# A reordered first batch, shifted pieces and later query loads in a cosformer attention and mixer kernel

## The chip, the cores and the metric

The kernel runs on one core of a Trainium2 chip. Its engines work side by side, each through its own list of instructions in order: PE (TensorE, matmuls, with its weight loads listed as PEld), DVE (VectorE), ACT (ScalarE), POOL (GpSimd) and SP (SyncE, which here only issues transfers). Sixteen DMA engines move data. The metric is the device time of one execution in microseconds (us), as the median of several runs.

## The reference

Inputs are q, k and v of shape 8 x 8 x 576 x 64 (batch, heads, sequence, head width) and four weight matrices. Attention is linear: a feature map, two sums over the sequence, a quotient. Then comes a mixer over tokens and one over channels.

```python
def phi(x, c, s):
    r = np.maximum(x, 0.0)
    return np.concatenate([r * c, r * s], axis=-1)
q_p, k_p = phi(q, cos_w, sin_w), phi(k, cos_w, sin_w)   # cos, sin of pi/2 * pos / 576
kv = np.einsum('bhsf,bhsd->bhfd', k_p, v)
z = np.sum(k_p, axis=2)
num = np.einsum('bhsf,bhfd->bhsd', q_p, kv)
den = np.einsum('bhsf,bhf->bhs', q_p, z)[..., None] + 1e-06
x = (num / den)                                          # to (batch, 576, 512)
h = np.maximum(x.transpose(0, 2, 1) @ w_tok1, 0.0) @ w_tok2
u = x + h.transpose(0, 2, 1)
out = u + np.maximum(u @ w_ch1, 0.0) @ w_ch2             # w_ch1 512x1536, w_ch2 1536x512
```

## The kernel before, in words

The 576 positions of a batch are four full chunks of 128 (ci 0 to 3) and a tail of 64 (ci = R = 4). The tails of two batches share one set of 128-row tiles (the class Tail): the even batch has rows 0 to 63, the odd one rows 64 to 127.

Each batch has a front and a channel part. The front makes the features (`feature`, by `k_side` and `q_side`: one cosine and one sine operation for a chunk), casts the values into `v_aug` with a column of ones (`values`), transposes the query features (`q_trans` on PE, or `q_trans_dma` by a DMA that SP issues), sums kv (`kv`, copied out by `kv_out`), forms the numerator (`num`, which ends in the DVE operation that writes x), and mixes tokens (`tok1`, `tok1_out`, `tok2`, which writes u; `u_trans_dma` then transposes u). The channel part (class Channel) has twelve `c_main` steps, each four matmuls and a relu on ACT into h1T, and then o steps of two matmuls each, whose sums DVE adds to u and SP stores.

The order is written out by hand; nothing reorders it. The first batch's front (`first_front`) runs alone at the start, with filler matmuls (`busy`) that keep PE occupied. After it, while one batch's channel part runs, the pieces of the next batch's front are issued between its steps: `pieces` returns a plan of (slot, what, arguments), where the slot counts the channel steps (C = 0 for the c_main steps, O = 12 for the o steps), and the main loop calls them after that step. A negative slot lies at the end of the batch before. The plan has one form for the second batch (`first`), one for the third (`late`), one for odd and one for even batches. Whatever is issued takes its place in its engine's list, so a piece that waits holds up what stands behind it on that engine, though not other engines.

Loads are issued by SP, one also by ACT at the start, and the casting loads of the channel weights by POOL. The main loop places the loads of later batches by step number (`load_batch`, at the end of the kernel). SP also issues the stores and the DMA transposes, so these too stand in its order. Every buffer is a pool tile with a fixed number of copies: four PSUM tiles of one bank (`ps_mm`), two of two banks (`ps_at`); a matmul group waits until the tile's last reader is done.

In the first batch's front the denominators of all chunks are computed ahead, from the key sums (`ksum`, `ksum_out`, `dens`, `dens_out`): dens of three chunks, then the first half (four heads) of kv, then dens of the other two, then the second half of kv. The two token weights are loaded as f32 into buffers that later hold u, and are cast (`cast_tok1`) or permuted (`permute_tok2`) on ACT; the tail rows of the first token weight come by two casting loads on POOL (L183). The fills of ones and zeros of both copies of `v_aug` and `x_tail` are on DVE (L158 to L163).

The lines of the plan that the text refers to most are those of the second batch:

```python
plan = [(4, KS, 0), (4, KS, 1), (5, u, 0, ps_at, False), (5, KS, 2, True),
        (6, KS, 3, True), (6, u, 1, ps_at, False), (7, KS, R), (7, V, R, nc.vector), (8, V, 0, act),
        (8, V, 2, pool), (8, load_w_ch2, 0), (8, V, 3, pool),
        (8, load_w_ch2, 1), (8, load_w_ch2, 2),
        (8, u, 2, None, False), (9, V, 1, act), (9, u, 3, None, False),
        (9, QS, 0), (10, u, R, None, False)]
```

Here `u` is the first batch's own `tok2`: its u is finished beside its own channel part, since its channel input was formed on PE directly (`turned_x`, `turned_b`).

Of the kernel before, what the change touches and what calls it, by code (L numbers as in the profile page):

```python
# [16 lines left out]
def kernel(  # L17
# [137 lines left out]
    v_augs, x_tails = [], []  # L155
    for i in range(2):
        va = const.tile([P, NSC, H, DP], BF16, name=f"v_aug{i}")
        nc.vector.memset(va[:, 0:R, :, D:D1], 1.0)  # L158
        nc.vector.memset(va[half(1 - i), R, :, :], 0.0)
        nc.vector.memset(va[half(i), R, :, D:D1], 1.0)  # L160
        v_augs.append(va)
        xt = const.tile([P, Dm], BF16, name=f"x_tail{i}")
        nc.vector.memset(xt[half(1 - i), :], 0.0)  # L163
        x_tails.append(xt)
# [29 lines left out]
    def load_w_ch2(third):  # L194
        ki = third * NCH // 3
        w_ch2_done.append(nc.gpsimd.dma_start(
            out=w_ch2[:, ki:ki + 4, :],
            in_=moe_w_ch2[ki * P:(ki + 4) * P, :].rearrange("(n t) d -> t n d", t=P)))
# [10 lines left out]
    def permute_tok2(ki):  # L209
        nc.scalar.copy(w_tok2[:, ki, 0:SM].rearrange("t (r p) -> t r p", r=R),  # L210
                       w_tok2n[:, ki, 0:SM].rearrange("t (p r) -> t r p", r=R))
        nc.scalar.copy(w_tok2[:, ki, SM:].rearrange("t (g s) -> t g s", g=2),
                       w_tok2n[:, ki, None, SM:S].to_broadcast([P, 2, ST]))


    class Front:
        def __init__(self, b, res, tail):
            self.qt, self.vt, self.kt = io_tiles[b]
            self.va, self.xt = v_augs[b % 2], x_tails[b % 2]
            self.res, self.tail = res, tail  # L220
            self.rows = half(b % 2)


            self.alone = b < 2
            self.kp, self.qp = {}, {}
# [69 lines left out]
        def dens(self, ci):  # L295

            if ci == 0:
                self.d_ps = ps_mm.tile([P, NSC * H], F32, name="d_ps", tag="mm")
                self.d_sb = small.tile([P, NSC * H, 1], F32, name="d_sb")
            for h in range(H):  # L300
                i = ci * H + h
                nc.tensor.matmul(self.d_ps[:, i:i + 1], self.qT_of(ci, h),
                                 self.ks_sb[:, h:h + 1], start=True, stop=True)

        def dens_out(self, lo, hi):
            nc.vector.tensor_scalar_add(self.d_sb[:, lo:hi, 0], self.d_ps[:, lo:hi], 1e-6)
            nc.vector.reciprocal(self.d_sb[:, lo:hi, 0], self.d_sb[:, lo:hi, 0])

        def kv(self, ci, halves=(0, 1)):
            if ci == 0 and not hasattr(self, "kv_ps"):  # L310
                self.kv_ps = {}
                if halves == (0, 1):
                    both = ps_at.tile([P, 2, 512], F32, name="kv_ps", tag="at")
                    self.kv_ps = {g: both[:, g, :] for g in range(2)}
            if ci == 0 and halves != (0, 1):
                for g in halves:
                    self.kv_ps[g] = ps_at.tile([P, 2, 512], F32, name="kv_ps", tag="at")[:, 0, :]
# [10 lines left out]
        def kv_out(self, halves=(0, 1)):  # L328
            for g in halves:
                copy = nc.vector.tensor_copy if g else nc.scalar.copy  # L330
                copy(self.kv_sb[g][:, :, 0:D1],  # L331
                     self.kv_ps[g][:, 0:HH * DP]
                     .rearrange("p (j d) -> p j d", d=DP)[:, :, 0:D1])
# [13 lines left out]

        def q_trans_dma(self, ci):
# [4 lines left out]
        def num(self, ci, fill=0, dens=False):  # L353
            num_ps = ps_at.tile([P, 2, 512], F32, name="num_ps", tag="at")
            if fill:
                busy(num_ps[:, 0, HH * DP:512], 1)
            for h in range(H):
                g, j = divmod(h, HH)
                nc.tensor.matmul(num_ps[:, g, j * DP:j * DP + D1], self.qT_of(ci, h),  # L359
                                 self.kv_sb[g][:, j, 0:D1], start=True, stop=True)  # L360
            rows = self.rows_of(ci)
            nv = num_ps[rows, :, 0:HH * DP].rearrange("p g (j d) -> p g j d", d=DP)
            if dens:
                den = self.d_sb[rows, ci * H:(ci + 1) * H, :].rearrange("p (g j) o -> p g j o", g=2)
            else:
# [3 lines left out]
            nc.vector.tensor_mul(  # L369
                self.x_of(ci)[rows].rearrange("p (g j d) -> p g j d", g=2, j=HH),  # L370
                nv[:, :, :, 0:D], den.to_broadcast([rows.stop - rows.start, 2, HH, D]))
# [89 lines left out]
        def pieces(self, b, before):  # L461
# [7 lines left out]
            if first:  # L469

                u, act, pool = before.tok2, nc.scalar, nc.gpsimd
                plan = [(4, KS, 0), (4, KS, 1), (5, u, 0, ps_at, False), (5, KS, 2, True),
                        (6, KS, 3, True), (6, u, 1, ps_at, False), (7, KS, R), (7, V, R, nc.vector), (8, V, 0, act),
                        (8, V, 2, pool), (8, load_w_ch2, 0), (8, V, 3, pool),
                        (8, load_w_ch2, 1), (8, load_w_ch2, 2),
                        (8, u, 2, None, False), (9, V, 1, act), (9, u, 3, None, False),
                        (9, QS, 0), (10, u, R, None, False)]
# [6 lines left out]
            else:  # L484
                plan = [(C + at, V, ci, nc.scalar)
                        for ci, at in enumerate((6, 6, 7, 7, 7) if late else (-1, -1, 0, 1, 2))]

                if odd:
# [8 lines left out]
                for at, side, ci in sides:  # L497
                    plan.append((C + at, side, ci))
                    if side == QS:
# [3 lines left out]
                         enumerate((7, 7, 8, 8, 8) if late else  # L503
# [28 lines left out]
    class Channel:  # L532
# [59 lines left out]
        def steps(self, done):  # L592
# [43 lines left out]
    def first_front(f):  # L636
# [26 lines left out]
        busy(idle_ps, 1)  # L663
        for ci in range(R):
            if ci == 2:
                f.ksum_out()
            f.values(ci, nc.scalar, lo_heads)
        cast_tok1(0)
        f.values(R, nc.vector)
        for ci in range(R):  # L670
            f.values(ci, nc.vector, hi_heads)
        for ci in (0, 1, 2):
            f.dens(ci)
# [15 lines left out]
        f.num(ORDER[0], fill=1, dens=True)  # L689
        f.num(ORDER[1], dens=True)  # L690
# [57 lines left out]
    for b in range(B):  # L748
# [4 lines left out]
        for i, step in enumerate(steps):  # L753
# [54 lines left out]
```

## Time and profile before

| what | value |
|---|---|
| median of three runs | 270.0 us (269.47 to 270.21) |
| the profiled execution | 270.61 us |
| its span | 268.8 us |
| PE busy | 260.0 us, 97% |
| DVE busy | 164.9 us, 61% |
| ACT busy | 129.9 us, 48% |
| POOL busy | 10.9 us, 4% |
| DMA queue of SP | 49.62 MB, 69.5% of the 16 engines' span |
| granted PE clock | full speed throughout |

The span is what the profile shows; the profiled execution's own time is 1.80 us more, and 0.61 us above the median. A busy PE is not PE at its peak, since the ends of its matmuls are modelled; but steps that follow each other without a wait show how long a stretch must take. A wait is given in brackets behind a row with what ended it. A row with a count above one merges instructions that follow each other on one engine.

### The profile page before, as it was taken

The numbers are of one execution on the slowest core, as the hardware profiler recorded it, in microseconds if no ns is written. First come the engines' busy times: TensorE is split into PE (matmuls) and PEld (weight loads), VectorE is DVE, ScalarE is ACT, GpSimd is POOL, SyncE is SP. The second block draws the span as 40 slices with busy tenths as digits, with TensorE's granted clock in tenths as the row PEclk, the third lists the DMA queues.
The fourth block names the chain that finished last, engine by engine and source line by source line (L and its number), as shares of the span: only waits on it lengthen the run. The fifth ranks groups of instructions, "written<-read, shape, count | busy, mean of one in ns | idle before, by whom it ended". The sixth has DMA issues, their size and how long they took to land.

```text
span 268.8 us, 5101 instructions
## 1 busy us (share of the span) xinstructions
PE 260.0 (97%) x2029; PEld 139.2 (52%) x2050; DVE 164.9 (61%) x376; ACT 129.9 (48%) x228; POOL 10.9 (4%) x24
## 2 busy tenths in 40 slices
PE   7989999999999999999999999999999999999994
PEld 2565465455544455446644455446644455445543
DVE  6874798794366747777466747776565846720022
ACT  4954975528606272446606372546606362526400
POOL 6300220000000000000000000000000000000000
PEclk9999999999999999999999999999999999999999
DMA  6999999589999999469984989189974580180032
GB/s 217 342 277 275 333 162 285 211 210 253 179 316 289 251 208 319 146 166 266 182 307 117 287 207 355 54 179 254 229 261 117 156 120 0 53 202 3 2 107 88
DMA packets 91815, 53.68 MB, mean 200 GB/s; under 512 B 59408, under 2 KB 86928, under 8 KB 91792
## 3 DMA queue, kind: packets, MB, share of 16 engines
q1 hardware_dynamic: 88432, 49.62, 69.5%
q0 software_dynamic: 2832, 3.21, 7.2%
q10 hardware_dynamic: 528, 0.52, 0.6%
q8 instruction: 16, 0.26, 0.4%
q14 instruction: 7, 0.06, 0.1%
HBM read 35.85 MB, written 9.44 MB: 168 GB/s over the span
## 4 chain that ended last, share of the span: by engine, by line
PE 86%; DVE 6%; DMA 3%; ACT 3%; issue 1%; DVEq 0%; ACTq 0%
PE o_ps L579 33%; PE c_ps L546 25%; PE u_ps L406 7%; PE b_ps L382 6%; PE ct_ps L566 3%; PE kv_ps L320 3%; PE num_ps L359 3%; DVE x_sb L369 3%; DMA qt<-in_q_dram 2%; DVE qp L263 1%; ACT h1T L550 1%; PE qT_ps L340 1%; DMA qpT_tail<-qp_tail 1%; PE idle_ps L204 1%; ACT v_aug L274 1%; PE c_ps L556 1%
## 5 line engine op out<-in xcount | busy, mean ns | idle before, releaser
L579 PE MATMUL o_ps<-w_ch,h1T 128*128 128x512 bf16 (+1 forms) x380 | 92.6, 372 | 0.6
L546 PE MATMUL c_ps<-uT,w_ch 128*128 128x512 bf16 (+2 forms) x384 | 92.2, 372 | 0.1
L550 ACT ACTIVATE h1T<-c_ps 128x512 bf16<-128x512 f32 x93 | 55.5, 599 | 60.5 <-PE c_ps L546 60.1
L579 PEld LDWEIGHTS <-h1T 128*128 128x128 bf16 x396 | 37.3, 98 | 39.5 <-issue 0.2
L546 PEld LDWEIGHTS <-w_ch 128*128 128x128 bf16 x384 | 33.5, 97 | 29.5 <-issue 0.2
L584 DVE TENSOR_TENSOR o_sb<-o_ps,u_sb 128x512 f32<-128x512 f32 (+1 forms) x33 | 22.3, 674 | 29.5 <-PE o_ps L579 29.4
L409 DVE TENSOR_TENSOR u_sb<-u_ps,x_sb 128x512 f32<-128x512 f32 x32 | 21.7, 689 | 6.0 <-PE u_ps L406 5.6
L413 ACT CAST u_bf<-u_sb 128x512 bf16<-128x512 f32 x28 | 17.3, 620 | 16.7 <-DVE u_sb L409 16.7
L406 PE MATMUL u_ps<-B,w_tok 128*128 128x512 bf16 x79 | 22.4, 379 | 0.2
L387 ACT ACTIVATE B<-b_ps 128x512 bf16<-128x512 f32 x8 | 4.8, 598 | 33.7 <-PE b_ps L382 33.5
L369 DVE TENSOR_TENSOR x_sb<-num_ps,den 128x512 bf16<-128x512 f32 x28 | 19.4, 691 | 1.0
L566 PEld LDWEIGHTS <-w_ch 128*128 128x128 bf16 x192 | 14.0, 98 | 9.2
L382 PE MATMUL b_ps<-x_sb,w_tok 128*128 128x512 bf16 x63 | 17.7, 379 | 0.1
L263 DVE TENSOR_SCALAR kp<-kt,cos_t 128x512 bf16<-128x512 f32 x32 | 15.2, 481 | 3.8 <-DMA kt<-in_k_dram 3.8
L566 PE MATMUL ct_ps<-uT_tail,w_ch 128*128 128x128 bf16 x192 | 17.2, 219 | 0.0
L274 ACT CAST v_aug<-vt 128x512 bf16<-128x512 f32 (+1 forms) x30 | 16.8, 587 | 0.1
L263 DVE TENSOR_SCALAR qp<-qt,cos_t 128x512 bf16<-128x512 f32 (+1 forms) x35 | 15.9, 455 | 0.5 <-DMA qt<-in_q_dram 0.5
L263 DVE TENSOR_SCALAR qp<-qt,sin_t 128x512 bf16<-128x512 f32 (+1 forms) x35 | 15.9, 455 | 0.0
L359 PEld LDWEIGHTS <-qpT 128*128 128x128 bf16 x256 | 11.5, 98 | 6.1 <-issue 1.1
L584 DVE TENSOR_TENSOR o_sb<-o_ps,u_tail 128x512 f32<-128x512 f32 x4 | 2.8, 692 | 19.0 <-PE o_ps L579 19.0
L359 PE MATMUL num_ps<-kv_sb,qpT 128*128 128x65 bf16 x256 | 13.0, 193 | 1.3 <-DVE x_sb L369 0.5
L331 DVE CAST kv_sb<-kv_ps 128x260 bf16<-128x260 f32 x8 | 3.5, 433 | 16.6 <-ACT kv_sb L331 16.5
(93 smaller groups left out, 228.6 us busy)
## 6 DMA issues: line engine op xcount, KB each, us to landing
out_dram<-o_sb SPq DMA_DIRECT2D x31, 256.0 KB, 2.9
kt<-in_k_dram SPq DMA_DIRECT2D x7, 1024.0 KB, 6.6
vt<-in_v_dram SPq DMA_DIRECT2D x7, 1024.0 KB, 6.6
qt<-in_q_dram SPq DMA_DIRECT2D x7, 1024.0 KB, 8.4
w_ch<-in_moe_w_ch_dram POOLq DMA_DIRECT2D x4, 384.0 KB, 10.2
w_ch<-in_moe_w_ch_dram POOLq DMA_DIRECT2D x3, 512.0 KB, 7.5
out_dram<-o_sb SPq DMA_DIRECT2D x10, 128.0 KB, 2.3
qtt<-in_q_dram SPq DMA_DIRECT2D x8, 128.0 KB, 5.3
```

What stands on the lines that cost most here:

```text
L263: nc.vector.tensor_scalar(o_ap, i_ap, scalar1=w, scalar2=0.0, op0=ALU.mult, op1=ALU.max)
L274: nc.scalar.copy(dst, src)
L359: nc.tensor.matmul(num_ps[:, g, j * DP:j * DP + D1], self.qT_of(ci, h), self.kv_sb[g][:, j, 0:D1], start=True, stop=True)
L369: nc.vector.tensor_mul(self.x_of(ci)[rows].rearrange("p (g j d) -> p g j d", g=2, j=HH), nv[:, :, :, 0:D], den.to_broadcast([rows.stop - r ...
L382: nc.tensor.matmul(self.b1_ps[mi], w, self.x_of(ci), start=(ci == ORDER[0]), stop=(ci == ORDER[-1]))
L406: nc.tensor.matmul(u_ps, w_tok2[:, ki, ci * P:(ci + 1) * P], self.B1[:, ki, :], start=(ki == 0), stop=(ki == NT - 1))
L409: nc.vector.tensor_add(u, u_ps[rows], self.x_of(ci)[rows])
L546: nc.tensor.matmul(c_ps[:, lo:hi], w_ch1[:, ki, mi * P:(mi + 1) * P], uT[:, lo // P:hi // P, ki, :], start=(ki == 0), stop=(ki == NCC - 1))
L550: nc.scalar.activation(self.h1T[:, mi, :], c_ps, AF.Relu)
L566: nc.tensor.matmul(self.ct_ps[:, mi % R, :], w_ch1[:, ki, mi * P:(mi + 1) * P], self.tail.uT[:, ki, :], start=(mi % R == 0 and ki == 0), s ...
L579: nc.tensor.matmul(o_ps, h, w_ch2[:, ki, cols], start=ki == 0, stop=ki == NCH - 1)
L584: nc.vector.tensor_add(o_sb, o_ps, u)
```

## The change

It has three parts.

In the first batch's front: the tail rows of the first token weight are loaded by SP as f32, behind the main part and ahead of the second token weight, and cast by POOL. Half of the second token weight is permuted by POOL instead of ACT, and the fixed fills of the second `v_aug` and `x_tail` move from DVE to POOL, after that. The tail's queries are transposed on 64 rows only. The sine features of key chunks 1 to 3, instead of 2 and 3, are on ACT. Filler matmuls are fewer between key sums. The values of chunks 0 and 1 are cast on DVE and of 2 and 3 on ACT. All dens are computed in one go ahead of both kv halves, the kv halves have PSUM tiles of their own, both are copied out by ACT, and the nums of the first two chunks are formed by halves, the first of them in `ps_mm` tiles.

In the plans: the second batch's key, value and first query pieces come one or more slots later, behind u pieces of the first batch, which come earlier. The second channel weight is loaded in four pieces instead of three, and the first batch's o steps alternate after every step instead of every second one. The third batch's values and kv come one or two slots earlier. The fourth batch has all its key features before its query features, and these later.

In the loads: the third batch's value tails come with its values, its query tails later, in the second batch's stage; the fourth batch's queries are loaded in that stage's o steps, and the fifth batch's keys at the second step of the third batch's channel part.

```diff
@@ the first loads
+    w_tail1n = stage1[:, R * D_tok:(R + 1) * D_tok]
     nc.sync.dma_start(out=w_tok1n, in_=moe_w_tok1[0:SM, :].rearrange("(p r) t -> p r t", r=R))
+    for g in range(2):
+        nc.sync.dma_start(out=w_tail1n[half(g), :], in_=moe_w_tok1[SM:S, :])
     nc.sync.dma_start(out=w_tok2n, in_=moe_w_tok2.rearrange("(n t) s -> t n s", t=P))
...
-    for t in (tail0.kp, tail0.qp):
-        nc.gpsimd.memset(t[half(1)], 0.0)
-    for g in range(2):
-        nc.gpsimd.dma_start(out=w_tail1[half(g), :], in_=moe_w_tok1[SM:S, :])
+    nc.gpsimd.memset(tail0.kp[half(1)], 0.0)
+    nc.gpsimd.memset(tail0.qpT[:, :, half(1)], 0.0)
@@ first_front
-        f.q_trans(R, pool=ps_at)
-        busy(idle_ps, 2)
+        f.q_trans_tail_first()
+        busy(idle_ps, 3)
         for ci in range(R):
             f.feature("k", ci, 0)
-            f.feature("k", ci, 1, on_act=(ci > 1))
-            busy(idle_ps, 2)
+            f.feature("k", ci, 1, on_act=(ci > 0))
+            busy(idle_ps, 1)
             f.ksum(ci)
...
-        for ci in (0, 1, 2):
-            f.dens(ci)
+        den = f.dens(range(NSC))
+        f.dens_out(*den)
         for ci in range(NSC):
             f.kv(ci, (0,))
         f.kv_out((0,))
-        for ci in (R, 3):
-            f.dens(ci)
-        f.dens_out(0, NSC * H)
         for ci in range(NSC):
             f.kv(ci, (1,))
-        f.kv_out((1,))
-        cast_tok1(1)
-        for ki in range(NT):
-            permute_tok2(ki)
+        f.kv_out((1,), on_act=(1,))
+        for ci in ORDER[:2]:
+            f.num(ci, dens=True, halves=(0,), pool=ps_mm, fill=1)
+        for ci in ORDER[:2]:
+            f.num(ci, dens=True, halves=(1,), fill=1)
+        for mi in range(NT):
+            cast_tok1(mi)
+        permute_tok2(0, nc.scalar.copy)
+        nc.gpsimd.tensor_copy(w_tail1, w_tail1n)
+        permute_tok2(1, nc.gpsimd.tensor_copy)
+        fill_fixed(1, nc.gpsimd)
@@ pieces, the second batch
+                plan = [(4, u, 0, ps_at, False), (5, u, 1, ps_at, False), (6, u, 2, None, False),
+                        (6, KS, 0), (6, KS, 1), (7, u, 3, None, False), (7, KS, 2, True),
+                        (8, u, R, None, False), (8, KS, 3, True), (9, KS, R),
+                        (9, V, R, nc.vector), (9, V, 0, act),
+                        (10, V, 2, pool), (10, load_w_ch2, 0, 2), (10, V, 3, pool),
+                        (10, load_w_ch2, 2, 4), (10, load_w_ch2, 4, 8),
+                        (10, load_w_ch2, 8, NCH), (10, V, 1, act), (11, QS, 0, True)]
@@ pieces, later batches
-                        for ci, at in enumerate((6, 6, 7, 7, 7) if late else (-1, -1, 0, 1, 2))]
+                        for ci, at in enumerate((4, 5, 6, 6, 7) if late else (-1, -1, 0, 1, 2))]
+                if b == 3:
+                    sides = ((-4, KS, 0), (-3, KS, 1), (0, KS, 2), (1, KS, 3),
+                             (2, QS, 0), (3, QS, 1), (4, QS, 2), (5, QS, 3))
...
-                         enumerate((7, 7, 8, 8, 8) if late else
+                         enumerate((6, 7, 7, 8, 8) if late else
@@ the first batch's o steps
-                for lo in range(0, NCH, 4):
+                for lo in range(0, NCH, 2):
                     for ci in (0, 1):
-                        o_range(ci, lo, lo + 4)
+                        o_range(ci, lo, lo + 2)
@@ the main loop
             if b == 0 and i == NCH:
-                load_batch(2, "kq", behind=w_ch2_done[1], tails=False)
+                load_batch(2, "kq", behind=w_ch2_done[2], tails=False)
             if b == 0 and i == NCH + 13:
-                load_batch(2, "v", tails=False)
-                load_batch(2, "kqv", main=False)
+                load_batch(2, "v")
+                load_batch(2, "k", main=False)
+            if b == 1 and i == 3:
+                load_batch(2, "q", main=False)
             if b == 1 and i == 9:
-                load_batch(3, "kvq")
+                load_batch(3, "kv")
+            if b == 1 and i == NCH + 12:
+                load_batch(3, "q")
+            if b == 2 and i == 1:
+                load_batch(4, "k")
             if 1 < b < B - 2 and i == NSC:
                 load_batch(b + 2, "vq")
-            if 0 < b < B - 3 and i == NCH + 12:
+            if 1 < b < B - 3 and i == NCH + 12:
                 load_batch(b + 3, "k")
```

More of the change, by code (lines that the diff above doesn't have):

```diff
@@ L152, with fill_fixed @@
     nc.gpsimd.memset(ones[half(1), 1:2], 0.0)
[L155 to L164, printed above, removed]
+    v_augs = [const.tile([P, NSC, H, DP], BF16, name=f"v_aug{i}") for i in range(2)]
+    x_tails = [const.tile([P, Dm], BF16, name=f"x_tail{i}") for i in range(2)]
+    def fill_fixed(i, eng):
+        va = v_augs[i]
+        eng.memset(va[:, 0:R, :, D:D1], 1.0)
+        eng.memset(va[half(1 - i), R, :, :], 0.0)
+        eng.memset(va[half(i), R, :, D:D1], 1.0)
+        eng.memset(x_tails[i][half(1 - i), :], 0.0)
+    fill_fixed(0, nc.vector)
     class Tail:
@@ L346, in q_trans, with q_trans_tail_first @@
                 nc.vector.tensor_copy(dst, qT_ps)
+        def q_trans_tail_first(self):
+            qT_ps = ps_mm.tile([P, H, ST], BF16, name="qT_ps", tag="mm")
+            for h in range(H):
+                nc.tensor.transpose(qT_ps[:, h, :],
+                                    self.tail.qp[half(0), h, :, :].rearrange("p a b -> p (a b)"),
+                                    ident[half(0), half(0)])
+            nc.scalar.copy(self.tail.qpT[:, :, half(0)], qT_ps)
         def q_trans_dma(self, ci):
@@ L351, in q_trans_dma, with num @@
                                         in_=self.q_of(ci).rearrange("p h a b -> p (h a b)"))
[L353 to L362, printed above, removed]
+        def num(self, ci, dens=False, halves=(0, 1), pool=ps_at, fill=0):
+            shape, tag = ([P, 2, 512], "at") if pool is ps_at else ([P, 1, 512], "mm")
+            num_ps = pool.tile(shape, F32, name="num_ps", tag=tag)
+            busy(num_ps[:, 0, HH * DP:512], fill)
+            for g in halves:
+                for j in range(HH):
+                    nc.tensor.matmul(num_ps[:, g - halves[0], j * DP:j * DP + D1],
+                                     self.qT_of(ci, g * HH + j),
+                                     self.kv_sb[g][:, j, 0:D1], start=True, stop=True)
+            rows, n = self.rows_of(ci), len(halves)
+            nv = num_ps[rows, 0:n, 0:HH * DP].rearrange("p g (j d) -> p g j d", d=DP)
             if dens:
-                den = self.d_sb[rows, ci * H:(ci + 1) * H, :].rearrange("p (g j) o -> p g j o", g=2)
+                den = self.d_sb[ci][rows].rearrange("p (g j) o -> p g j o", g=2)
+                den = den[:, halves[0]:halves[-1] + 1]
             else:
```

84 lines of the change are left out of this document (36 added, 48 removed).

## The prediction

> **What bounds the kernel now.** I read the page first (busy shares, slices, the chain that ended last), then the busy time by stage, then the waits and the order of time inside the three stages that the change touches.
>
> ```profile
> span 268.8 us, 5101 instructions
> PE 260.0 (97%) x2029; PEld 139.2 (52%) x2050; DVE 164.9 (61%) x376; ACT 129.9 (48%) x228; POOL 10.9 (4%) x24
> ...
> DMA  6999999589999999469984989189974580180032
> ...
> PE 86%; DVE 6%; DMA 3%; ACT 3%; issue 1%; DVEq 0%; ACTq 0%
> ```
>
> TensorE (PE) is the bound almost everywhere, so only its waits, and the front in which it runs filler, can be won or lost. The DMA engines are as full as PE for the first third of the span, which is where loads move. The stages, each from one batch's first channel matmul to the next batch's (columns: window, its length, PE busy, and so on):
>
> ```profile
> 26.70:56.30 29.60, 29.39 (x233) 15.94 (x236) 24.71 (x53) 18.57 (x29) 3.55 (x5) 1.00 0.95 244
> 56.30:91.00 34.70, 33.60 (x266) 18.44 (x268) 20.86 (x47) 16.11 (x29) 0.00 (x0) 1.00 1.00 250
> 91.00:118.70 27.70, 27.59 (x196) 13.88 (x197) 18.86 (x42) 13.71 (x24) 0.00 (x0) 1.00 0.95 224
> 118.70:151.40 32.70, 32.59 (x256) 17.65 (x256) 20.93 (x47) 14.96 (x27) 0.00 (x0) 1.00 0.80 216
> ```
>
> The second batch's stage (56.3 to 91.0) takes 2.0 us more than its like, the fourth's (118.7 to 151.4). The starts of its matmuls show where: 0.71 us at the kv matmuls (65.0 to 67.6, behind the value casts on ACT), 0.61 before the first num at 70.62, 0.38 before the tail's num at 74.57: 1.7 us is all that can be won there. The first and third batches' stages hold no wait. The last two waits, from the waits of that stretch, are for transposes by DMA:
>
> ```profile
> PEld L359 <- DMA qpT_tail<-qp_tail: 0.7, 1, 0.7
> PEld L359 <- DMA qpT<-qp: 0.6, 1, 0.6
> ```
>
> The last view is DVE and POOL in the first batch's stage, in order of time:
>
> ```profile
> 28.43 0.49 DVE L263 TENSOR_SCALAR kp<-kt,cos_t 128x512 bf16<-128x512 f32 x1 [3.09 <-DMA kt<-in_k_dram]
> ...
> 32.86 0.83 DVE L263 TENSOR_SCALAR kp_tail<-ktt,sin_t 64x512 bf16<-64x512 f32 x1
> ...
> 33.37 0.79 POOL L276 CAST v_aug<-vt 128x512 bf16<-128x512 f32 x1
> 33.62 0.83 DVE L276 CAST v_aug<-vtt 64x512 bf16<-64x512 f32 x1
> ...
> 38.80 0.43 DVE L331 CAST kv_sb<-kv_ps 128x260 bf16<-128x260 f32 x1
> ```
>
> From the landing of the second batch's keys (28.41) DVE has no gap up to 40 us; it is the hidden second bound of this stage.
>
> **The change part by part.** Sums are against the profiled execution: 270.61 us, 1.80 around the span of 268.81, and 0.61 above the median 270.0 of the three times shown.
>
> *The front, -0.4.* The keys' sine features 1 to 3 go to ACT. ACT's eight qpT copies end at 10.60; the tail's copy halves (1.01 for 128x1024, so about 0.51); three sines at 0.76 follow and end at 13.45, against 13.19 for two before. PE has one filler instead of two between key sums (0.22 less each): the last key sum moves from 14.31 to about 14.13, and the dens from 14.90 to 14.72. They are now all 40 (0.025 us each by 24 in 0.60), so the first kv half starts 0.22 later, but nothing stands between the halves, and the second half's copy runs on ACT at 17.15 instead of on DVE at 17.32. The halved nums let DVE begin x at 17.4 instead of 18.12; four halves at 0.35 (128x260 casts take 0.43 with 0.08 of tail) and three wholes at 0.63 bring the last x to 20.95 against 21.35. From there all is as before: -0.39. Ends: +0.3, if POOL's new work is late. It copies w_tail1 (behind w_ch1's issue, which ends at 14.1) and permutes half of w_tok2 after that lands (19.1, perhaps 0.4 later behind two more loads on SP's queue). ACT takes 1.11 + 0.30 for it, POOL's plain cast 0.60 to ACT's 0.62; even twice ACT's time ends at 22.3, where turned_b first needs it. Lower end -0.7, if the keys land earlier without the two w_tail loads beside them. The four fixed fills moved from DVE to POOL stood in DVE's wait for q (4.0 to 4.9) and gain nothing; the removed qp_tail fill and w_tail1 issues on POOL stood before its wait for the keys.
>
> *The first batch's stage, +1.4.* Pieces of the second batch move behind the first one's u adds. The durations of the rows, put in the new order, each engine in order and a PSUM buffer free only when its reader is done, give before's stage to 0.1 us, and for the new order this: DVE is idle until the first u (29.1 instead of starting keys at 28.43) and for 0.6 us between u0, u1 and u2, because each waits for PE; keys start at 32.3, just when POOL's casts stretch DVE's SBUF operations (0.83 for 0.48 above). So u3's add ends at 35.5 and c_main 10, which needs its PSUM buffer, waits 0.58. ACT's sines and value casts now follow h 7 to 10 with no gap from 32.5 to 38.2; the second value chunk is ready at 37.7 and kv waits 0.29. The first query's sine (ACT, behind h 11) ends at 39.0: its transposes wait 0.41; the tail's wait 0.15. Sum 1.44. Who waits is PE, with the o steps queued behind. Ends: 0.6 (no PSUM wait, POOL's stretch gone) to 1.8 (two more w_ch2 issues on POOL stretching DVE too).
>
> The Trainium skill's GPSIMD Engine Reference (Performance pitfalls for Q7 kernels) has POOL sharing its SBUF interfaces with DVE operations that use two ports; the 0.83 us rows agree. By it the x operations, which read PSUM, are not stretched by POOL's new work in the front, and the -0.39 stands.
>
> *The second batch's stage, +0.6.* Value casts one or two slots earlier, with the values' tails now first in the queue, remove the 0.71. The queries' tails are now issued behind the third query transpose. In DVE's order qp_tail stands ahead of the kv copy, which the first num needs. Landings on SP's queue keep the order of issue throughout, so the tails land behind that transpose. It landed at 72.45; two tail loads fewer ahead take 0.82 off (64.14 to 64.96), the two put behind add 0.9: 72.5. But in that stretch the DMA packets stop twice, from 66.1 to 68.0 and 68.9 to 70.4. Without either it is 69.1; with one of 1.1 us (the mean of the twenty such stops over 0.6 us in the trace's DMA packets, the longest 1.9) it is 70.2, which I take. Then two features (0.88 to DVE's next) and the copy (0.49): the first num at 71.6 against 70.62, +0.95; the tail's transpose, issued at 71.1 and landing 2.9 later, is in time, -0.38. Ends: -0.5 (no stop) and +2.9 (both).
>
> *The third batch's stage, +1.3.* The fourth batch's queries are loaded behind the transposes of u instead of in the stage before, and the fifth's keys behind them: both stand ahead of the four query transposes. Counting from the landing of uT at 88.70: 1 MB 3.7 us (the packets of vt, 58.4 to 62.1), 768 KB of output 2.25, 1 MB 3.7, two tails 0.9, one transpose 0.95: 100.2, against the num at 100.03, which now waits 0.2; with the same stop of 1.1, 1.3. Ends 0 (uT no longer queues behind the queries' load that landed at 85.18) and 2.9 (the two stops that this stretch had, 1.4 each). DVE's later query features end near 97.3, before its kv copy at 99.2: hidden by that wait. w_ch2 in four pieces lands its first quarter before its first user at 39, and the o steps alternate to match: nothing.
>
> Sum: -0.39 + 1.44 + 0.57 + 1.3 = +2.9; 273.5 for a profiled execution, **272.9** on the median.
>
> **The rivals.** *Not slower: the queries' tails and the fourth batch's transposes come in time.* Place: the second batch's first num. If its tails land by 67.9 in before's times (1.37 ahead of a num at 69.3), all 1.69 us of waits go, and with free queues the third stage loses nothing: -0.39 + 1.44 - 1.69 = -0.6, 269.4. For: some stages have no long stop. Against: order of issue, and 1 us for each transpose.
>
> *The first stage absorbs its pieces* (DVE and ACT catch up, as POOL's casts move with them): 0 for 1.44, 271.5. For: DVE holds 24.7 us of work in 29.6. Against: its work is in one block, before kv.
>
> *Full stops.* Both in each stage: 2.9 + 2.9 + 1.05 = +6.8, 276.8. For: this is what the trace of before shows. Against: such stops were shorter in the fifth and later stages.
> The trace's own rows have PE slow after idleness: the first twelve fillers take 4.16 us, four later ones 0.86, though the granted clock reads 1.00. The Trainium skill, TensorE: Matmul & The Clock Gate (HAM oscillation), says that an idle gap of about 3.4 us halves the clock; gaps of 1 to 2 us, as I forecast, would not. A wait of 4.5 us here would: about 8 matmuls at 0.43 for 0.215 more, an estimate of +1.7 by the fillers' rows. No run here shows it in mid-kernel yet.
>
> *POOL late in the front*: its permutation at three times ACT's: +0.9 beside the rest, 273.8.
>
> **How the numbers follow.** Forecast 0.45 (271.5 to 274.3), in time 0.2, absorbed 0.15, full stops 0.15, POOL late 0.05. The range 269.7 to 276.0 leaves out the better half of the in-time case and the worse half of the full stops. About 0.3% (0.8 us) is what a measurement can tell from no change. Faster: half of in time, 0.1. Same: the other half and a fifth of absorbed, 0.13. Slower 0.77.
>
> **What would show it.** After: the last x of the front near 20.95; DVE idle beside u0 to u2 and PE waiting at c_main 10, kv and the first query's transposes; qp_tail on DVE waiting for qtt, with the first num behind; the fourth batch's first num waiting for qpT. I am wrong if DVE's kv copy in the second stage isn't behind a wait for qtt, or if the first stage stays near 29.6 us.

## The result and the profile after

The changed kernel takes 280.3 us (median of four runs, 277.65 to 281.09), the kernel before 270.1 (269.47 to 270.24): a ratio of 1.0365, interval 1.0294 to 1.0436. It is slower, as forecast, but by 10.2 us where the forecast had 2.9; the time lies outside the range. The profiled execution is the shortest of the four, 277.65 us with a span of 275.8. The other three took 280.1 to 281.1 at a mean granted clock of 0.988, the profiled one at 0.994, before at 1.000. That difference turns out to be a cause.

The page of the changed kernel: span, busy shares, the granted clock and the DMA share in 40 slices, and the chain that ended last by engine.

```profile
span 275.8 us, 5128 instructions
PE 263.5 (96%) x2049; PEld 140.4 (51%) x2049; DVE 163.4 (59%) x371; ACT 129.2 (47%) x229; POOL 13.2 (5%) x30
...
PEclk9999999999989999999999999999999999999999
DMA  7999999589792899978991899659993681171022
...
PE 81%; DVE 6%; DMA 6%; SPq 3%; ACT 3%; issue 1%; POOL 0%; DVEq 0%; POOLq 0%
```

PE has lost 5 points of the chain, to DMA and to SP's queue, and one slice shows a clock below full. To see where, I cut the span at the first channel matmul of each batch. Busy time by stage of the changed kernel (window, length, PE busy and so on, PEclk, DMA share, GB/s):

```profile
24.03:57.52 33.49, 32.73 (x248) 17.24 (x247) 25.21 (x54) 19.48 (x31) 4.32 (x6) 1.00 0.94 242
57.52:95.43 37.91, 34.89 (x269) 19.48 (x268) 20.66 (x47) 15.85 (x29) 0.00 (x0) 0.95 0.81 200
95.43:125.65 30.22, 27.75 (x198) 13.53 (x197) 18.96 (x42) 13.69 (x24) 0.00 (x0) 1.00 0.91 239
125.65:158.40 32.75, 32.75 (x258) 17.65 (x257) 20.91 (x47) 14.94 (x27) 0.00 (x0) 1.00 0.79 213
```

| part, cut the same way in both | before | after | difference | forecast |
|---|---|---|---|---|
| front | 24.45 | 24.03 | -0.42 | -0.39 |
| first batch's stage | 31.89 | 33.49 | +1.60 | +1.44 |
| second batch's stage | 34.70 | 37.91 | +3.21 | +0.57 |
| third batch's stage | 27.50 | 30.22 | +2.72 | +1.3 |
| all after | 150.27 | 150.20 | -0.07 | 0 |

The sum is +7.04 for the profiled executions; the median of after lies 2.65 above its profiled execution, and that of before 0.50 below its own. All of the 7.04 lies in three stages, and two of them were sized far too small. In the second batch's stage, PE in order of time:

```profile
70.64 0.39 PE L581 MATMUL ct_ps<-uT_tail,w_ch 128*128 128x128 bf16 x4
70.87 0.28 PE L368 MATMUL num_ps<-kv_sb,qpT 128*128 128x65 bf16 x4
73.90 0.28 PE L368 MATMUL num_ps<-kv_sb,qpT 128*128 128x65 bf16 x4 [2.75 <-DVE kv_sb L331]
74.01 1.40 PE L561 MATMUL c_ps<-uT,w_ch 128*128 128x512 bf16 x4
75.21 1.49 PE L581 MATMUL ct_ps<-uT_tail,w_ch 128*128 128x128 bf16 x12
76.49 0.65 PE L368 MATMUL num_ps<-kv_sb,qpT 128*128 128x65 bf16 x8
```

and DVE at the same time:

```profile
72.62 0.49 DVE L264 TENSOR_SCALAR qp_tail<-qtt,cos_t 128x512 bf16<-128x512 f32 x1 [6.16 <-DMA qtt<-in_q_dram]
73.02 0.48 DVE L264 TENSOR_SCALAR qp_tail<-qtt,sin_t 128x512 bf16<-128x512 f32 x1
73.42 0.42 DVE L331 CAST kv_sb<-kv_ps 128x260 bf16<-128x260 f32 x1
```

The first four matmuls of the num go, those of the second half wait for DVE's kv copy, which stands behind the features of the query tails, which wait 6.16 us for their load: the place that the forecast named, with 2.91 us between the starts that surround it. What follows is new. The twelve tail matmuls from 75.21 take 1.28 us to the next start, 0.107 each; at 68.69 four channel matmuls took 0.87, and 128 columns at that pace are 0.054. PE runs at half speed there. The busy time by windows, cut where the clock's records change, shows it:

```profile
71.11:74.53 3.42, 0.68 (x9) 0.40 (x7) 1.50 (x5) 0.33 (x1) 0.00 (x0) 1.00 0.59 108
74.53:77.94 3.41, 3.41 (x26) 2.34 (x25) 1.48 (x5) 1.20 (x2) 0.00 (x0) 0.50 0.77 192
77.94:81.35 3.41, 3.41 (x38) 1.90 (x36) 2.77 (x10) 0.00 (x0) 0.00 (x0) 1.00 1.06 362
```

A window in which PE was almost idle (0.68 us busy) is followed by one at clock 0.50, then full speed again. Added up over the starts of the matmuls, the half clock costs about 1.5 us. The stage's +3.21 is thus, within 0.1, 2.91 of the new wait, 0.37 of a kv wait that stayed, 1.5 of the clock, less the 1.5 of waits over 0.2 us that before had here.

In the third batch's stage the first num of the fourth batch starts at 107.05, 2.64 us late. PE's waits in that stretch:

```profile
PE num_ps L368 <- DMA qpT<-qp: 2.5, 1, 2.5
```

Again the place is the forecast's. The transpose was issued at 99.45, SP's queue took 5.60 us to accept it, and it landed at 107.01, behind the fourth batch's queries (landed 97.87), stores (100.77) and the fifth batch's keys (105.35, tails 106.33).

### The profile page after: what moved, and what is told of

It is laid out like the page before. It is cut to its first block, busy times and chain, and to the rows that moved or that the text cites. A ratio compares the mean times of both kernels' runs of the same rounds, so it can differ in the third digit from the quotient of the medians.

```text
span 275.8 us, 5128 instructions
## 1 busy us (share of the span) xinstructions
PE 263.5 (96%) x2049; PEld 140.4 (51%) x2049; DVE 163.4 (59%) x371; ACT 129.2 (47%) x229; POOL 13.2 (5%) x30
## 4 chain that ended last, share of the span: by engine, by line
PE 81%; DVE 6%; DMA 6%; SPq 3%; ACT 3%; issue 1%; POOL 0%; DVEq 0%; POOLq 0%
PE o_ps L594 32%; PE c_ps L561 23%; PE b_ps L393 6%; PE u_ps L417 5%; PE num_ps L368 4%; PE ct_ps L581 3%; DMA qpT<-qp 3%; PE kv_ps L320 2%; PE idle_ps L205 2%; DMA ktt<-in_k_dram 2%; ACT qpT L344 1%; DVE kp L264 1%; DMA qtt<-in_q_dram 1%; SPq L92 1%; DVE u_sb L420 1%
## 5 line engine op out<-in xcount | busy, mean ns | idle before, releaser
L594 PE MATMUL o_ps<-w_ch,h1T 128*128 128x512 bf16 (+1 forms) x396 | 94.6, 374 | 0.0
L561 PEld LDWEIGHTS <-w_ch 128*128 128x128 bf16 x384 | 33.5, 97 | 29.6 <-issue 0.2
L581 PEld LDWEIGHTS <-w_ch 128*128 128x128 bf16 x192 | 14.7, 101 | 9.5 <-issue 0.5
L368 PE MATMUL num_ps<-kv_sb,qpT 128*128 128x65 bf16 x256 | 13.6, 195 | 5.6 <-DVE kv_sb L331 2.7
L581 PE MATMUL ct_ps<-uT_tail,w_ch 128*128 128x128 bf16 x192 | 17.9, 225 | 0.0
L264 DVE TENSOR_SCALAR kp<-kt,cos_t 128x512 bf16<-128x512 f32 x32 | 16.0, 505 | 0.1
L378 DVE TENSOR_SCALAR den<-num_ps 128x8 f32<-128x8 f32 (+1 forms) x35 | 5.8, 165 | 14.0 <-PE num_ps L368 13.8
```

The costliest lines, as they stand in the source:

```text
L264: nc.vector.tensor_scalar(o_ap, i_ap, scalar1=w, scalar2=0.0, op0=ALU.mult, op1=ALU.max)
L368: nc.tensor.matmul(num_ps[:, g - halves[0], j * DP:j * DP + D1], self.qT_of(ci, g * HH + j), self.kv_sb[g][:, j, 0:D1], start=True, stop=True)
L561: nc.tensor.matmul(c_ps[:, lo:hi], w_ch1[:, ki, mi * P:(mi + 1) * P], uT[:, lo // P:hi // P, ki, :], start=(ki == 0), stop=(ki == NCC - 1))
L581: nc.tensor.matmul(self.ct_ps[:, mi % R, :], w_ch1[:, ki, mi * P:(mi + 1) * P], self.tail.uT[:, ki, :], start=(mi % R == 0 and ki == 0), s ...
L594: nc.tensor.matmul(o_ps, h, w_ch2[:, ki, cols], start=ki == 0, stop=ki == NCH - 1)
```

## The experiments

The first four runs shared a chip and runs of before with a median of 269.9 us; for the others the median of before is given with each. The base is the changed kernel ("after") unless a heading says otherwise.

### Which load makes which wait: the query tails back

```diff
-                load_batch(2, "k", main=False)
-            if b == 1 and i == 3:
-                load_batch(2, "q", main=False)
+                load_batch(2, "kq", main=False)
```

> Only the loads of the third batch's query tails go back to where they stood, with its key tails at the end of the first batch's stage. Queue order is the cause (theory): in the trace of after the first num waits 2.91 us behind DVE's features of the query tails, and PE then runs 3.3 us at half clock, which costs 1.65; both go, the transposes land 0.9 later. Second batch's stage 39.4 -> 37.9 at least without the clock's loss and 35.5 to 36.5 in all; the third stage keeps its wait on qpT. Median 280.3 less 3 to 4.5: 275.3 to 277. Stops of the transfers are the cause (rival): the first num then waits for the first transpose instead, 2 us or more remain, and the median stays above 278.5.

Measured: 276.7 us (275.57 to 278.27); ratio 1.0258 (1.0217 to 1.0299). The 2.91 us wait is gone, and the first num starts behind a wait of 0.49. The second stage takes 34.43 us. So the tails' place in the queue carries that stage's loss, 3.6 us on the median. The third stage takes 33.60 us: it kept its wait, which was 4.45 us in this profile, and behind it stands another window at half clock, which makes up the other 1.65 over the 27.50 of before (two windows of the busy time, before and behind the wait's end):

```profile
103.51:106.92 3.41, 0.80 (x11) 0.55 (x12) 0.31 (x2) 0.00 (x0) 0.00 (x0) 1.00 1.27 161
106.92:110.33 3.41, 3.41 (x24) 1.79 (x22) 1.81 (x5) 1.00 (x2) 0.00 (x0) 0.50 0.87 223
```

The wait is longer than in after mostly because the transfers stop once more: from 104.05 us the queue moves next to nothing for 1.3 us, and the first transpose lands 2.28 us behind the key tails instead of 0.68. What makes the transfers stop is not shown; in the second stage of four profiles the stop begins 0.3 to 0.7 us after a packet of 16 KB on the instruction queue does (68.3 and 67.86 in after). This is what I take the median of after to hold beyond its profile: the wait in the third stage is at times longer, and then has a half clock too. Two such windows in 279 us are a mean clock of 0.988, one is 0.994, as the runs have it. There is no second profile of after itself to show it; the rival is a second window in the front, where three other profiles with the new front have one. The fillers below speak against it.

### The fourth batch's queries and the fifth's keys back

```diff
-                load_batch(3, "kv")
+                load_batch(3, "kvq")
             if b == 1 and i == NCH + 12:
-                load_batch(3, "q")
-            if b == 2 and i == 1:
                 load_batch(4, "k")
```

> Only the loads of the fourth batch's queries and the fifth's keys go back to the second batch's stage. Queue order is the cause (theory): the 2.64 us wait of the third stage's first num goes; the third stage takes 27.5 to 27.8 instead of 30.22. The median of after is 2.65 above its profiled execution and its mean clock 0.988 instead of 0.994, which I read as a second stretch at half clock behind a longer wait there; with that gone the median is 274.5 to 275.5 at a clock of 0.994. Stops are the cause (rival): a wait of 2 us or more at the first num of the third stage remains and the median stays above 278. If the second stretch at half clock is not tied to that wait, the clock stays 0.988.

Measured: 275.4 us (273.89 to 275.46); ratio 1.0192 (1.0161 to 1.0223). The third stage has no wait left and takes 27.50 us, as in before. The median falls by 4.9 us: the 2.7 of after's profile, and some 2.2 of what its other runs had beyond it. The profiled execution is the shortest of the four by 1.5 us; what the others had more is in no trace. In it the second stage's wait stayed, 2.95 us, but here no half clock followed it. The one window at half clock of this profile is in the front, from 15.24 us. The two windows that share the 2.95 us wait of this kernel:

```profile
69.90:73.30 3.40, 1.82 (x18) 1.13 (x17) 0.08 (x1) 1.68 (x3) 0.00 (x0) 1.00 1.06 222
73.30:76.70 3.40, 2.20 (x30) 1.61 (x30) 2.31 (x7) 0.95 (x2) 0.00 (x0) 1.00 0.37 83
```

The clock's records change only at multiples of 3.41 us from each other in every profile, and the grid lies differently in each execution. Here the wait fell across a border, so that neither window was idle enough.

### Both back

The two edits above together.

> Both loads back where they stood; the front and the shifted pieces stay. If the loads carry the loss alone, what is left is the front's -0.42, the first stage's +1.60 and whatever the second stage's earlier value casts win (0 to 1.2): 270 + 1.2 - (0 to 1.2) = 270.0 to 271.2, clock 1.000. If the pieces carry part of it (rival), a wait of over 1 us stays in the second or third stage and the time is above 272.

Measured: 271.7 us (271.10 to 272.73); ratio 1.0073 (1.0045 to 1.0100). The stages take 33.70, 34.20 and 27.50 us. Of the 10.2 us, the loads carried 8.6 (3.6 and 4.9 alone); what is left is the first stage. It is a little above the expected range: the second stage won 0.5 in the profile, and the first took 1.81 more than in before, where 1.60 was expected.

### PE kept busy in the waits

```diff
+            if ci == ORDER[0]:
+                fill += {2: 26, 3: 24}.get(self.b, 0)
             busy(num_ps[:, 0, HH * DP:512], fill)
```

> After, with 26 filler matmuls of 252 columns (0.105 us each, 2.73 us) ahead of the third batch's first num and 24 (2.52 us) ahead of the fourth's; no wait is taken away, PE is only kept busy in them. If idleness of PE is what halves the clock (theory): the clock reads 1.000, the first num still starts near 73.9 and the fourth's near 105.3, and the median falls by 1.65 for each stretch, 280.3 to about 277.0. If the half clock has another cause (rival: the burst of work behind the wait, or the transfers): the clock stays 0.988 to 0.994 and the time stays within 1 us of 280.3.

Measured: 277.0 us (276.48 to 277.93), clock 1.000 in three of four runs and 0.994 in one. The fillers have 192 columns, not 252, so they fill 2.1 and 1.9 us; that was enough. PE in order of time, second stage:

```profile
71.35 2.31 PE L205 MATMUL num_ps<-zeros,ident 128*128 128x192 bf16 x26
73.49 0.28 PE L370 MATMUL num_ps<-kv_sb,qpT 128*128 128x65 bf16 x4
74.33 0.28 PE L370 MATMUL num_ps<-kv_sb,qpT 128*128 128x65 bf16 x4 [0.55 <-DVE kv_sb L331]
```

The second half of the num still starts 0.43 later than in after, the fourth batch's first at 106.52. The waits are all there, filled with useless work, and 3.3 us are gone: two windows' worth. So the half clock comes from PE's idleness in the waits, not from the transfers or from what follows. The front is the one of after, so the two windows that three of after's four runs had most likely lay behind these waits, and not in the front.

### The front alone (base: before)

All of the change's front, with the plans and loads of before.

> Before with the new front only; plans and loads as before. The front's part by the trace of after is -0.42: 269.5 against 269.9. But the front of the two kernels with loads put back began its channel part 0.95 later in two of three profiles, behind a stretch of 3.41 us at half clock that begins at 14.9 or 15.4 us; the windows of 3.41 us ahead of those held 2.3 and 2.5 us without streaming columns, in the other profiles 2.15 or less (before: 1.8). If the thinner filler does this (theory), runs fall in two groups, near 269.5 and near 270.5, and the median lies between; if it came from the loads behind, all runs are at 269.5.

Measured: 270.05 us (269.02 to 270.96, 12 runs), before 270.09 (23 runs); ratio 0.9999 (0.9980 to 1.0017). The two groups are there. Six runs with a clock of 0.997 or more took 269.02 to 270.17, mean 269.69; six with 0.991 to 0.994 took 270.03 to 270.96, mean 270.49. So where the clock holds, the front gains about 0.4, as in the profile, and the other half of the executions lose 0.8, twice the gain, to what their clock shows as one window. The profiled execution is one of the first group; three other profiles with this front show the window in it, where there are fewer fillers between the key sums. Here it is in the kernel with the query tails back:

```profile
11.35:14.76 3.41, 2.90 (x58) 1.70 (x55) 2.99 (x10) 2.33 (x6) 2.06 (x3) 1.00 1.09 343
14.76:18.17 3.41, 3.41 (x80) 3.40 (x78) 0.60 (x2) 1.51 (x5) 0.39 (x1) 0.50 1.11 278
```

The window ahead counts as 2.90 us busy, but most of its 58 instructions are matmuls of one column (eight for each key sum). Counted by the columns that stream (0.213 us for 512), 2.33 of its 3.41 us are without any.

### The shifted pieces alone (base: before)

The new plan of the second batch with its four loads of the second channel weight and the alternating o steps.

> Before with the second batch's new plan only (u pieces first, the four loads of the second channel weight, the alternating o steps). If the shifted pieces make the first stage's +1.6 (theory): first channel matmul of the second batch 1.6 to 1.8 later than in before, waits at kv and the query transposes that sum to 1.4 to 1.7, time 271.4 to 271.8. If the new front makes it (rival: its later casts of the token weights and fills on POOL): 270.0.

Measured: 271.7 us (271.47 to 273.53), before 270.09; ratio 1.0079 (1.0050 to 1.0108). Busy time of its first stage:

```profile
24.25:57.58 33.33, 32.59 (x244) 17.15 (x246) 24.92 (x54) 19.43 (x31) 4.39 (x6) 1.00 0.93 239
```

33.33 against 31.89 is +1.44, the forecast's number to the last digit, though its waits are not the four of the forecast's sum (see the account below).

### Fillers again in the front (base: before with the new front)

```diff
             f.feature("k", ci, 1, on_act=(ci > 0))
-            busy(idle_ps, 1)
+            busy(idle_ps, 2)
             f.ksum(ci)
...
         f.ksum(R)
+        busy(idle_ps, 1)
         f.ksum_out()
```

> The new front alone with two fillers again between key sums and one ahead of the denominators. They fit into waits of 0.27 and 0.39 us, so the front keeps its -0.42 by the theory, and no window of 3.41 us is without streaming for more than 1.6 us: clock 1.000 in every run, 269.5. If the fillers are on the path (as I reckoned in the forecast, 0.22 each ahead of the key sums): 269.8 to 270.0 in every run.

Measured: 270.3 us (269.10 to 272.17); ratio 1.0006 (0.9985 to 1.0028). The clock was 0.999 or more in all twelve runs: the fillers do hold it. The time did not follow; the channel part began at 24.56 in the profile. One of the fillers stands ahead of the first key sum, on the path, so a second form has two only ahead of the later key sums:

```diff
-            busy(idle_ps, 2)
+            busy(idle_ps, 1 + (ci > 0))
```

> The new front alone, with the second filler only ahead of the second to fourth key sums and one ahead of the denominators: there PE waits 0.27 and 0.39 us. The full set of fillers had one more ahead of the first key sum, 0.21 on the path. Theory (idle windows): clock 0.997 or more in all runs, channel part begins within 0.1 of the front alone (23.9 to 24.2), 269.5 to 269.8 against 270.1. If more filler costs its own time: 270.1 or more.

Measured: 270.2 us (269.59 to 272.34), before 269.76; ratio 1.0022 (1.0003 to 1.0040), clock 0.997 or more in all twelve. In its profile the channel part began at 25.09, behind a gap of 0.77 us ahead of the first token matmul for which the trace names no releaser, and a transposition of the query tails 0.47 later than with the front alone. Whether the fillers cause that I can't say: in the three profiles with such fillers (the third is that of the last run below) the clock also rose to full only at 7.1 to 7.4 us, in the others with the new front at 4.1 to 6.8. In the old front a late rise cost nothing: 7.17 us in one profile (the earlier value casts, below), 4.24 in that of before, and both begin the channel part at 24.45. What full clock in the front is worth stays open.

### The fifth batch's keys behind the transposes (base: the query tails back)

```diff
-            if b == 2 and i == 1:
-                load_batch(4, "k")
             if 1 < b < B - 2 and i == NSC:
-                load_batch(b + 2, "vq")
+                load_batch(b + 2, "kvq" if b == 2 else "vq")
```

> The kernel with the query tails early, and the fifth batch's keys loaded behind the four query transposes instead of ahead of them; the fourth batch's queries stay late. If the bytes ahead in the queue are what makes the wait (theory): 1.3 MB less ahead is 4.6 us, as long as the wait of 4.45 us there, which goes to 0.5 or less, with the half clock behind it: 276.7 less 4.5 to 6: 270.7 to 272.2, as with both loads early. If the queries' own late load makes it: 2 us or more of wait stays, 273.5 or above.

Measured: 273.6 us (273.27 to 276.43), before 270.09; ratio 1.0158 (1.0115 to 1.0201). The wait at the fourth batch's first num is gone altogether. But the third stage still isn't free and takes 28.96 us: its end waits for the transposes of u, in PE's waits from 105 to 123 us:

```profile
PE c_ps L561 <- DMA uT<-u_bf: 1.3, 1, 1.3
```

The 1.3 MB that no longer stand ahead of the query transposes stand ahead of the next ones. Both theories missed a part: the bytes ahead do make the wait, and moving them moves it. With the queries loaded a stage earlier (both back) there is none.

### The query tails later, alone (base: before)

```diff
-                load_batch(2, "kqv", main=False)
+                load_batch(2, "kv", main=False)
+            if b == 1 and i == 3:
+                load_batch(2, "q", main=False)
```

> Before, with only the third batch's query tails loaded in the second batch's stage, behind the third query transpose. My forecast's size for it: first num 0.95 later, the tail's wait of 0.38 gone: 270.7. By the trace of after (theory now): DVE's kv copy waits for the tails, the first num waits 2 to 3 us in all instead of 0.61, +1.5 to +2.5, and in runs where a window of 3.41 us holds over 2.3 us of it another 1.65: median 271.5 to 274. If the first stage's lateness is needed for it (rival): 270 to 271.

Measured: 274.3 us (273.78 to 276.54), before 269.76; ratio 1.0188 (1.0155 to 1.0221), clock 0.992 to 0.994 in all four. PE's waits from 56 to 95 us, and DVE in order of time:

```profile
PE num_ps L359 <- DVE kv_sb L331: 3.0, 1, 3.0
```

```profile
71.72 0.49 DVE L263 TENSOR_SCALAR qp_tail<-qtt,cos_t 128x512 bf16<-128x512 f32 x1 [7.96 <-DMA qtt<-in_q_dram]
72.12 0.48 DVE L263 TENSOR_SCALAR qp_tail<-qtt,sin_t 128x512 bf16<-128x512 f32 x1
72.52 0.43 DVE L331 CAST kv_sb<-kv_ps 128x260 bf16<-128x260 f32 x1
```

Three lines of code cost 4.5 us by themselves, a little above the range expected, without any help of the other parts. The second half of the first num starts at 73.00 behind 3.12 us, and the second batch's stage takes 38.43 us.

### The earlier value casts alone, and a version of the parts that do no harm

Base before, with the third batch's value tails ahead of its others and its value casts and kv one or two slots earlier:

> Before, with only the third batch's value tails ahead of its other tails, its value casts and kv sums one or two slots earlier. Forecast: the waits at kv in the second stage (0.52 by stretches over 0.2) go, the waits for transposes stay: -0.3 to -0.7, 269.4 to 269.8. If kv merely waits at its earlier place (rival; after had 0.37 to 0.63 there): within 0.2 of before.

Measured: 269.8 us (269.28 to 270.26); ratio 0.9994 (0.9973 to 1.0015). The waits at kv are gone in the profile, as forecast, and the second stage takes 33.65 us. But that stage also takes 33.68 with the front alone, where its code is the old one, and 34.70 in the profile of before; it varies by 1 us with the landings of its transposes (before waits 0.61 and 0.38 us for them, the front alone does not), and no gain can be told.

The new front with the fillers of the second form, the old plan, all loads early, the earlier value casts and the new order of the fourth batch's features:

> The new front with fillers only where PE waits anyway, the old plan of the second batch, all loads early, and from the change only the earlier value casts and kv of the third batch and the order of the fourth batch's features. By the parts so far: front -0.4 to -0.6 without half clock, the second stage -0.5 (34.20 against 34.70 with both loads early): 0.9 to 1.1 less than before, 269.0 to 269.2 against 270.1. If the parts only move waits along (rival): within 0.5 of before.

Measured: 270.5 us (269.73 to 271.03), before 269.76; ratio 1.0016 (0.9998 to 1.0033). The rival was right: no combination that was run beats the kernel before by more than can be measured.

## Why the prediction was wrong in size

The place of each loss was right. What failed is the size of the waits in the second and third batches' stages, and the clock behind such a wait, which the sum had at nothing.

*The front, -0.39.* Right in the profile (-0.42), also by its steps: the last key sum at 14.09 (forecast 14.13), the last x at 20.93 (20.95). The contention of POOL and DVE that I cited from the Trainium skill's GPSIMD Engine Reference stands there in the section Key points; as I took from it, the x operation beside POOL's cast at 20.14 was not stretched (0.69 us, as the others). But the -0.39 was wrong as a time: alone the front measures 0.0, as half of the executions pay about 0.8 for a window at half clock. I had costed the removed fillers as 0.22 us each and at nothing else.

*The first batch's stage, +1.44.* Right: 1.60 in after, 1.44 alone. The mechanism was DVE's keys behind the u adds, and the trace of after has it, with DVE idle 0.45 and 0.60 us between u0, u1 and u2 and its first key feature at 32.18 (forecast 32.3). The list of waits was not: c_main 10 did not wait for its PSUM buffer (0.58 in the forecast), and instead kv waited 0.79 in two stretches (0.29) and the transposes 0.64 (0.41). All of them stem from the same late block, but that the errors cancel to the last digit is luck.

*The second batch's stage, +0.57.* This step failed. Its mechanism was right to the instruction: the first num behind the kv copy, behind the features of the query tails, behind their load. Its size was not, in two terms, which make up the 2.64 us that it was short by. The first is the tails' landing. The forecast had the num at 71.6, 15.26 us after the stage's start, with one stop of the transfers of 1.1 us; after has it at 16.38, with one stop of 1.3 (from 68.3). So it was the queue that was taken too fast. The forecast had the third transpose at 69.3 and two tails of 0.45, 70.2; the run of that part alone has 69.72 and 0.70 and 1.20, 71.62. From there to the num it is 1.38 us, as forecast (0.88 and 0.49). The second term is the clock, 1.5 us, which the sum left out. Of the 0.71 that was to go at kv 0.37 stayed, but that cost nothing: the load sets when the num starts, and without it the wait there would be that much longer.

*The clock.* I named the Trainium skill's rule (TensorE: Matmul & The Clock Gate, HAM oscillation) and set it aside with the sentence that gaps of 1 to 2 us, as I forecast, would not halve the clock. By the forecast's own terms PE was idle for 0.61 + 0.71 + 0.95 = 2.3 us at that num, so the gap was mis-stated, and the rule was read as a length of gap. The traces show windows: in the fourteen profiles, from the first full clock to the end of PE's work, every window with 2.19 us or more of its 3.41 without streaming columns was followed by one at half clock (2.19, 2.33, 2.53 twice, 2.66 and 2.80), and none with 2.15 or less was. Some matmul records can be missing, so the border is rough. Part 1 of the same page of the Trainium skill does say that the window is 4096 cycles long and free-running, which the grid in the traces agrees with; the idleness of about 3.4 us that it asks for was not needed in any of them. The price was worked out right, but only for a rival: +1.7 forecast for a wait of 4.5 us; measured are about 1.5 for one of 2.9 and 1.65 for one of 4.45.

*The third batch's stage, +1.3.* This step failed too: right place, half the size: 2.64 us in the profile, 4.45 in another, and by the clocks of the other runs a half clock behind it. Counted from the landing of uT, the forecast had 11.5 us and one stop of 1.1 to the first query transpose; it took 14.4, and between 93 and 105 us there was no stop. The queries took 5.3 us instead of 3.7 and the stores 2.9 instead of 2.25, while the keys and their tails took 5.6 instead of 4.6. I had added transfers at the speed that each has in a full queue.

*The rivals.* "Full stops" (276.8, chance 0.15) was the nearest number, but not by its mechanism: where it had two stops in each stage, after has one of 1.3 us in the second and none in the third's stretch. "Not slower" fell: with the tails placed late no run came in time. The parts alone measure 0.0, +1.6 and +4.5 us, and the third stage's loads 4.9 as what they cost in after; that makes 11.0 against 10.2 measured.

## What to carry to other kernels

A load that is placed "just in time" should be costed with the whole chain behind it on each in-order engine: three lines that moved two loads of 128 KB cost 4.5 us, because DVE's copy for the next matmul stood behind their user. When a queue is full, moving bytes behind one consumer puts them ahead of the next, as with the fifth batch's keys. And any wait of PE of 2 us or more, or several short ones that add up to it within a window as in the front, has a second price: work out how much of a 3.41 us window it can empty, and add about 1.5 us by the chance that it does.

## What the runs showed of the hardware

PE's clock is set in windows of 3.41 us on a grid that lies differently in each execution, and a window only about two thirds without streaming is enough to halve the next (2.19 us in the least, 2.15 in the most that was not). The same 2.9 us wait therefore costs 1.5 us more or nothing, by where it falls: 2.91 us was followed by half clock, 2.95 was not, as it lay across a border. One-column matmuls fill PE's busy time in the records but seem to count for little as activity: the front's window was 2.90 us busy by the profile and still halved the clock, while one of 1.61 us busy in after (from 105.25 us), with matmuls of 65 to 512 columns, did not. Fillers of 192 columns in a wait keep the clock up; they don't shorten the wait.
